# The product with the merged weights, as 36 matmuls a row tile or as seven products of quarter sums

## The chip, the cores and the metric

The kernel runs on one core of a Trainium2 chip. The metric is the device time of one execution in microseconds (us). The time before is 789.17 us, the median of three runs (788.98 to 789.34).

## The reference, cut to what matters

Three layers follow one another: an attention between 512 tokens and 32 state rows for each of 8 batches, a maximum of three products, and an exponential gate with a layer norm.

```python
scores = scale * np.matmul(x, state.transpose(0, 1, 3, 2))        # softmax(scores) @ state -> xread
...                                                               # the same the other way -> sread
x = np.ascontiguousarray(attn_out.transpose(0, 2, 1, 3)).reshape(B * S, H * D)
h = np.maximum(np.maximum(x @ w1, x @ w2), x @ w3)                # 512 -> 768
x = h @ w_out                                                     # 768 -> 512
h = x @ w_in                                                      # 512 -> 1024
e = np.exp(h - h_max)
sm = e / (np.sum(e, axis=-1, keepdims=True) + 1e-09)
solu = h * sm
ln = (solu - mu) / np.sqrt(var + 1e-06) * g_ln
return (ln @ w_out).astype(np.float32)                            # 1024 -> 512
```

Inputs and output are float32 (the weights come as float64 words and are cut down in the kernel). There are 4352 rows: 8 batches of 512 tokens, and 256 state rows.

## The kernel before, in words

Each float32 factor of a product is held as two float16 parts, a high part and the rest, and a product takes three matmuls (high-high, high-rest, rest-high: the pairs in `HL`). The two middle weights are merged first: W' = moe_w_out @ w_in, 768x1024, held in `Wp` as 6 slices `f` of 128 rows. So each row of h goes through one product with W' instead of two.

A batch goes through these steps. **Attention** (`x_*`, `sc_*`, `sn_*`): x is loaded into `xr` (one buffer), squared for its scale, split (`xh`), transposed by DMA (`xT`), multiplied with the state (`cP`, L288), and turned into attention weights `A` by a run of VectorE, ScalarE and GpSimd instructions (L298 to L375, the tiles `T`, `e2`, `A32`). **h**: for each of the 6 slices `f` the state times w1 to w3 is built (`uP`, L725, evacuated into `SW` at L731 and L734), and three matmul groups of six, one for each weight, give h (`hP`, L747). ScalarE scales the first (`hA`, L756), VectorE takes the maximum with the others (`hV`, `hW`, L762), ScalarE and GpSimd write the two float16 parts into `hT` (`hB`, L773, and `hG`, L777). **z**: for each of the 4 row tiles of 128 rows, `zP` (L805) runs 36 matmuls of 128x512 (6 slices, 3 pairs of parts, 2 column halves) into a double PSUM bank. Then come the row maximum on VectorE (`zM`, L814), the exponential on ScalarE (`zE`, L822), the product on VectorE (`zG`, L834), a square sum on ScalarE (`zQ`, L848), a small root on GpSimd (`zH`, L855 to L858), the high part on ScalarE (`zA`, L862), the normed value on VectorE (`zB`, L866), the rest on VectorE (`zC`, L871) and a DMA transposition (`zT`, L876). **Output**: `OP` (L886) runs 24 matmuls a tile, `OA` (L893) takes them out of PSUM and `OL` (L903) stores them. The 256 state rows go the same way as two tiles called `s`.

The order of all engines is written out by hand. `ORDER` is a string of words such as `zP:12` (step `zP`, batch 1, tile 2; in `hP:15` batch 1, slice 5), and every engine runs its instructions in the order in which the words stand:

```python
    with tc.manual_schedule():
        for word in ORDER.split():
            step(word)
```

Each engine waits in that order, so one waiting instruction holds all behind it. SP issues every load, store and transposition. PSUM has 8 banks: four single ones and two double ones (`bank`, `wide`). SBUF buffers that several steps share go by tag: `e` (6 buffers, for exponentials and weights in conversion), `hT`, `xr`, `hm`.

Of the kernel before, what the change touches and what calls it, by code (L numbers as in the profile page):

```python
# [981 lines left out]
```

## Time and profile before

| what | value |
|---|---|
| median of 3 runs | 789.17 us |
| the profiled execution | 788.87 us, its span 787.0 us |
| granted TensorE clock | 0.998 of full speed |
| TensorE busy | 761.6 us (97% of the span) |
| VectorE busy | 476.5 us (61%) |
| ScalarE busy | 383.3 us (49%) |
| GpSimd busy | 167.4 us (21%) |
| moved by DMA | 70.54 MB |

The profile of one execution gives a page (busy time of each engine, groups of instructions with their mean duration, DMA issues), and views of the trace: busy time in chosen windows, the chain of work that ended last, who waited for whom, and the instructions in order of time. The span is the time between the first and the last instruction of the core. The execution's own time is 1.9 us longer.

### The profile page before, as it was taken

To read this page: it belongs to the slowest core of one execution; us is meant where nothing else is said; L and a number is where in the kernel's file an instruction comes from. 1 tells how busy PE (TensorE), PEld (TensorE's weight loads), DVE (VectorE), ACT (ScalarE), POOL (GpSimd) and SP (SyncE) were. 2 spreads that over 40 slices of the span, in tenths; PEclk is the share of its full clock that TensorE was granted. 3 is DMA by queue.
4 is the path that set the end of the run, shared out by engine and by line. 5 is a ranking of instruction groups with operands and counts; after the bars stand their busy time and mean duration, and the time that the engine had idled before them with its cause. 6 is when DMAs were issued, how large, how long until landed. Compare 5 with 4: busy or idle time off the path is not lost.

```text
span 787.0 us, 12487 instructions
## 1 busy us (share of the span) xinstructions
PE 761.6 (97%) x5094; PEld 362.2 (46%) x5094; DVE 476.5 (61%) x840; ACT 383.3 (49%) x611; POOL 167.4 (21%) x222
## 2 busy tenths in 40 slices
PE   3898999999999999999999999999999999999998
PEld 1444444444444444444444444444444476444444
DVE  4689999986556546573755763647655534345261
ACT  5867768755345343644455444534543433153062
POOL 0012343133122220221211320223132112022020
PEclk9999999999999999999999999999999999999999
DMA  9997361430524131570451134610450401321144
GB/s 340 340 264 242 70 161 22 83 99 1 95 54 95 41 81 28 120 162 1 80 137 26 41 60 75 147 27 2 81 121 1 68 1 41 55 54 27 40 86 116
DMA packets 146729, 70.54 MB, mean 90 GB/s; under 512 B 127088, under 2 KB 135536, under 8 KB 146160
## 3 DMA queue, kind: packets, MB, share of 16 engines
q1 hardware_dynamic: 146672, 69.75, 37.3%
q8 instruction: 40, 0.66, 0.3%
q14 instruction: 17, 0.14, 0.1%
HBM read 29.89 MB, written 8.91 MB: 49 GB/s over the span
## 4 chain that ended last, share of the span: by engine, by line
PE 81%; DVE 8%; ACT 5%; DMA 3%; issue 1%; SPq 0%; POOL 0%; ACTq 0%; DVEq 0%; POOLq 0%
PE z L805 29%; PE o L886 21%; PE h L747 20%; PE hs L789 3%; PE sw L725 3%; PE zs L805 2%; DMA xr<-in_x_dram 2%; DVE cv L453 1%; PE os L886 1%; DMA raw<-in_moe_w_dram 1%; PE pr L388 1%; DVE Wt L649 1%; ACT cv L435 1%; ACT junk L462 1%; DVE SW L734 1%
## 5 line engine op out<-in xcount | busy, mean ns | idle before, releaser
L805 PE MATMUL z<-Wp,hT 128*128 128x512 f16 x1152 | 252.8, 379 | 0.0
L747 PE MATMUL h<-A,SW 128*128 128x512 f16 x864 | 192.6, 379 | 1.4 <-ACT SW L731 0.5
L805 PEld LDWEIGHTS <-hT 128*128 128x128 f16 x1152 | 111.9, 98 | 135.9 <-issue 2.5
L886 PE MATMUL o<-Wo,ln 128*128 128x512 f16 (+2 forms) x792 | 169.8, 373 | 0.4 <-DVE zsm L827 0.4
L747 PEld LDWEIGHTS <-SW 128*128 128x128 f16 x864 | 82.4, 98 | 103.8 <-issue 6.6
L886 PEld LDWEIGHTS <-ln 128*128 128x128 f16 x840 | 80.8, 98 | 95.5 <-issue 1.2
L777 POOL TENSOR_TENSOR hT<-hm,hT 128x512 f16<-128x512 f32 x48 | 59.5, 1248 | 190.7 <-ACT hT L773 173.7
L762 DVE SCALAR_TENSOR_TENSOR hm<-h,phi,hm 128x512 f32<-128x512 f32 x96 | 71.2, 747 | 38.5 <-ACT hm L756 35.6
L731 ACT ACTIVATE SW<-sw 128x384 f16<-128x384 f32 x96 | 44.4, 486 | 74.7 <-PE sw L725 56.9
L814 DVE TENSOR_REDUCE zmx<-z 128x1 f32<-128x1024 f32 x32 | 39.1, 1222 | 66.6 <-PE z L805 66.5
L734 DVE SCALAR_TENSOR_TENSOR SW<-sw,SW 128x384 f16<-128x384 f32 x96 | 51.8, 548 | 38.2 <-ACT SW L731 38.1
L822 ACT ACTIVATE e<-z,zmx,beta_x 128x1024 f32<-128x1024 f32 x32 | 38.5, 1202 | 70.0 <-DVE zmx L815 68.4
L893 ACT ACTIVATE ob<-o,gamma 128x512 f32<-128x512 f32 (+2 forms) x33 | 22.2, 672 | 102.5 <-PE o L886 90.1
L756 ACT ACTIVATE hm<-h,phi 128x512 f32<-128x512 f32 x48 | 32.8, 684 | 44.7 <-PE h L747 39.8
L855 POOL TENSOR_SCALAR rs<-rs 128x1 f32<-128x1 f32 x34 | 9.8, 289 | 208.5 <-ACT ln L848 208.5
L575 PE MATMUL wp<-Wo,Wp 128*128 128x512 f32 x96 | 46.5, 641 | 0.8 <-DVE Wo L453 0.8
L871 DVE TENSOR_TENSOR ln<-e,ln 128x1024 f16<-128x1024 f32 x34 | 44.3, 1306 | 0.3
L866 DVE TENSOR_SCALAR e<-e,mean,rs 128x1024 f32<-128x1024 f32 x34 | 30.5, 903 | 22.6 <-ACT ln L862 22.6
L862 ACT ACTIVATE ln<-e,nb,rs 128x1024 f16<-128x1024 f32 x34 | 41.9, 1235 | 3.4 <-POOL nb L858 3.4
L848 ACT ACTIVATE ln<-e,mean 128x1024 f16<-128x1024 f32 x34 | 38.8, 1143 | 9.6 <-DVE mean L837 6.0
L834 DVE SCALAR_TENSOR_TENSOR e<-z,zsm,e 128x1024 f32<-128x1024 f32 x32 | 40.9, 1279 | 0.6
L773 ACT CAST hT<-hm 128x512 f16<-128x512 f32 x48 | 29.1, 613 | 21.3 <-DVE hm L762 11.4
(151 smaller groups left out, 712.9 us busy)
## 6 DMA issues: line engine op xcount, KB each, us to landing
xr<-in_x_dram SPq DMA_DIRECT2D x8, 1024.0 KB, 6.4
out_dram<-ob SPq DMA_DIRECT2D x31, 256.0 KB, 3.2
raw<-in_moe_w_out_dram SPq DMA_DIRECT2D x5, 1024.0 KB, 6.0
raw<-in_moe_w_dram SPq DMA_DIRECT2D x4, 1024.0 KB, 12.2
Wt<-in_moe_w_dram SPq DMA_DIRECT2D x3, 1024.0 KB, 9.4
Wt<-in_moe_w_in_dram SPq DMA_DIRECT2D x2, 1024.0 KB, 7.1
raw<-in_moe_w_in_dram SPq DMA_DIRECT2D x2, 1024.0 KB, 10.1
raw_h<-in_moe_w_dram SPq DMA_DIRECT2D x2, 1024.0 KB, 10.0
```

The source lines that it names most:

```text
L575: nc.tensor.matmul(zs[f][:, c * HALF:(c + 1) * HALF], a1T[f][:, e], b1[:, e, c * HALF:(c + 1) * HALF], start=e == 0, stop=e == NE - 1)
L731: nc.scalar.activation(sw_t[b, f][:, 0, g], sw_t[b, f, g][:, :3 * P], AF.Copy, scale=2.0 ** -18)
L734: nc.vector.scalar_tensor_tensor(out=sw_t[b, f][:, 1, g], in0=sw_t.pop((b, f, g))[:, :3 * P], scalar=2.0 ** -18, in1=sw_t[b, f][:, 0, g], ...
L747: nc.tensor.matmul(parts[w], SW[:, u, g, w * P:(w + 1) * P], A[:, v, g, :], start=n == 0, stop=n == 3 * NG - 1)
L762: nc.vector.scalar_tensor_tensor(out=c, in0=h_t[b, f][i], scalar=phi[f // 2][:, i:i + 1], in1=c, op0=ALU.mult, op1=ALU.max)
L777: nc.gpsimd.tensor_tensor(out=h_t[b][:, 1, f, :n], in0=c_t.pop((b, f)), in1=h_t[b][:, 0, f, :n], op=ALU.subtract)
L805: nc.tensor.matmul(z[:, c * HALF:(c + 1) * HALF], h_t[b][:, u, f, t * P:(t + 1) * P], Wp[:, v, f, c * HALF:(c + 1) * HALF], start=n == 0, ...
L814: nc.vector.tensor_reduce(out=d["mx"], in_=d["z"], axis=AX.X, op=ALU.max)
L834: nc.vector.scalar_tensor_tensor(out=d["e"], in0=d["z"], scalar=d["sm"], in1=d["e"], op0=ALU.mult, op1=ALU.mult, accum_out=mu)
L862: nc.scalar.activation(d["ln"][:, 0, 0], d["e"], AF.Identity, bias=d["nb"], scale=d["rs"])
L871: nc.vector.tensor_tensor(out=d["ln"][:, 0, 1], in0=d["e"], in1=d["ln"][:, 0, 0], op=ALU.subtract)
L886: nc.tensor.matmul(d["po", c.start], lT[:, u, k, :], Wo[:, v, k, c], start=n == 0, stop=n == 3 * NK - 1)
```

## The change

For the batches 1 to 7 and for the state rows, z = h W' is no longer made tile by tile. h is taken as four quarters (even and odd slices `f`, first and second tile of a pair of row tiles `u`), W' as four quarters (even and odd slices, left and right 512 columns), and seven products of sums of quarters (`Y`, 9 matmuls of 128x512 each, into one bank) are added up to the four quarters of z. Batch 0 keeps the 36 matmuls a tile.

The words of the new steps: `j` sums of quarters of h on VectorE, `jA` and `jG` their two float16 parts on ScalarE and GpSimd; `t*` the sums of W', once, on GpSimd, ScalarE and VectorE, kept in `Ts` and in the upper right quarter of `Wp`; `Y:bui` product i of pair u of batch b; `K` the copy of product 1 into SBUF on ScalarE; `V` the additions on VectorE, the last one for each quarter with a row maximum; `wD` and `wR` write the converted w1 to w3 to DRAM and bring one third of them back for each batch, since `Ts` takes the room of one third.

Core of the diff (`ORDER` is written anew, with 1941 words for 1489; of it one line of each version stands here):

```diff
-zM:40 zE:40 eA:50 eA:51 zP:41 zR:40 uV:511 xP:6 zG:40 OL:31 n2:5 n3:5 eW:51 uA:500 uA:510 zM:41 n4:5
+uV:530 Y:406 hG:45 jG:400 jA:420 jG:420 uA:520 Y:403 Y:414 Y:405 K:40 Y:402 uV:520 zA:33 n3:5 zB:33
...
-    def bank(name):
-        return ps.tile([P, 512], F32, tag="bank", name=name, bufs=4)
-
-    def wide(name):
-        return ps.tile([P, 1024], F32, tag="wide", name=name, bufs=2)
+    free, held = list(range(8)), {}
+
+    def bank(name, uses=1):
+        k = free.pop(0)
+        t = ps.tile([P, 512], F32, tag=f"bank{k}", name=name)
...
+    def w_keep(q):
+        nc.sync.dma_start(out=W_mem[q], in_=Wq(0, q).rearrange("p v a i c -> p (v a i c)"))
+
+    def w_fetch(b):
+        q = order_q[b][2]
+        nc.sync.dma_start(out=Wq(b, q).rearrange("p v a i c -> p (v a i c)"), in_=W_mem[q])
...
-    NE4 = 6
+    NE4 = 5
...
+        half = NG * S
+        att_s[b] = {"xr": xr.rearrange("p (a j r d) -> p a j r d", a=NPR, j=2, d=D),
+                    "T": xr[:, :half].rearrange("p (g c n) -> p g c n", g=NG, n=N),
+                    "e2": xr[:, half:].rearrange("p (g s) -> p g s", g=NG), "A": xr[:, half:]}
...
+    def h_sum(b, q, i):
...
+        x, y, op = (lambda: (even(0), even(1), ALU.subtract), lambda: (even(1), odd(1), ALU.add),
+                    lambda: (t[:, 1], even(0), ALU.subtract), lambda: (odd(0), t[:, 2], ALU.subtract))[i]()
+        nc.vector.tensor_tensor(out=t[:, i], in0=x, in1=y, op=op)
...
+    TSUM = nc.gpsimd
...
+    def t_diff(q):
+
+        t = ts_t[q] = t_tile(q, "t32")
+        TSUM.tensor_tensor(out=t, in0=both(q, 1, 1), in1=both(q, 0, 1), op=ALU.subtract)
...
+    def y_mm(b, u, i):
+
+        y_t[b, u, i] = bank(f"y{b}_{u}_{i}", 2 if i == 5 else 1)
+        j, place = PRODUCTS[i]
+        n = 0
+        for q in range(NQ):
+            for v, w in HL:
+                nc.tensor.matmul(y_t[b, u, i], h_t[b][:, v, q, j, u * P:(u + 1) * P], place(w, q),
+                                 start=n == 0, stop=n == 3 * NQ - 1)
+                n += 1
...
+    SUMS = {6: (1, 0, 6, False), 2: (0, 0, 2, True), 7: (2, 1, 7, False), 8: (3, 2, 5, True),
+            5: (1, 1, 5, False), 3: (1, 1, 3, True), 4: (2, 2, 4, True)}
+
+    def y_add(b, u, i):
+
+        k, j, n, last = SUMS[i]
+        out_, x, y = z_half(b, u, k), z_half(b, u, j), y_t[b, u, n]
+        if last:
+            mh = z_t[b, 2 * u + k // 2]["mh"]
+            nc.vector.tensor_tensor_reduce(out=out_, in0=x, in1=y, scale=1.0, scalar=-3.0e38, op0=ALU.add,
+                                           op1=ALU.max, accum_out=mh[:, k % 2:k % 2 + 1])
+        else:
+            nc.vector.tensor_tensor(out=out_, in0=x, in1=y, op=ALU.add)
+        used(y)
...
     def z_norm(b, t):
         d = z_t[b, t]
-        nc.vector.tensor_scalar(out=d["e"], in0=d["e"], scalar1=d["mean"][:, 0:1], scalar2=d["rs"],
-                                op0=ALU.add, op1=ALU.mult)
+        nc.scalar.activation(d["e"], d["e"], AF.Identity, bias=d["nb"], scale=d["rs"])
```

Three places in the order show it. First VectorE in the middle of the run, at the gate of batch 3. `A32_4` belongs to the attention of batch 4, `z3_0` is the product of batch 3, tile 0; the last number of a name is its buffer. Before:

```order
L365 STREAM_TRANSPOSE A32_4_3642<-T4_3493 128x1024
L814 TENSOR_REDUCE zmx_3709<-z3_0_3604 128x1
L815 TENSOR_SCALAR zmx_3709<-zmx_3709,beta_x_93 128x1
L827 TENSOR_SCALAR zsm_3713<-zsm_3713,s_beta_x_950 128x1
L829 RECIPROCAL zsm_3713<-zsm_3713 128x1
L834 SCALAR_TENSOR_TENSOR e_3712,mu_3746<-z3_0_3604,zsm_3713,e_3712 128x1024
L837 TENSOR_SCALAR mean_3748<-mu_3746 128x1
L838 TENSOR_SCALAR mean_3748<-mu_3746 128x1
```

After, at the same place (`y3_0_6` is product 6 of pair 0 of batch 3, `zb` a row tile of z in SBUF):

```order
L1054 TENSOR_TENSOR zb_3876<-zb_3876,y3_0_6_3910 128x512
L1054 TENSOR_TENSOR zb_3945<-zb_3876,y3_0_7_3888 128x512
L1054 TENSOR_TENSOR zb_3876<-zb_3876,y3_0_5_3935 128x512
L831 SCALAR_TENSOR_TENSOR SW4_1_3696<-sw4_1_0_3697,SW4_1_3696 128x384
L831 SCALAR_TENSOR_TENSOR SW4_1_3696<-sw4_1_1_3698,SW4_1_3696 128x384
L1051 ISA zb_3945,zmh_3946<-zb_3945,y3_0_5_3935 128x512
L1051 ISA zmh_3946 128x1
L1051 ISA zb_3876,zmh_3877<-zb_3876,y3_0_3_3922 128x512
L1051 ISA zmh_3877 128x1
L1051 ISA zb_3945,zmh_3946<-zb_3945,y3_0_4_3964 128x512
L1051 ISA zmh_3946 128x1
L1137 TENSOR_TENSOR ln_3814<-e_3611,ln_3814 128x1024
```

The row maximum over 1024 columns (`L814`) is gone; the additions of the products stand in its place, and four of the seven carry a row maximum of 512 columns with them (`L1051`, and a row that reads it out).

Second GpSimd, in the stretch between batch 0's z and batch 1's. Before, it holds the softmax of batch 1 (`T`, `A`), the roots (`rs`, `nb`) and the rest parts of h (`hT`):

```order
L359 TENSOR_TENSOR T_1061<-T_1061,rn 128x1024
L708 TENSOR_SCALAR gamma<-p_o 128x1
L375 TENSOR_TENSOR A_1341<-A_1_1309,A_1341 128x1024
L262 TENSOR_SCALAR al_1380<-p_x_1375,p_s 128x1
L855 TENSOR_SCALAR rs<-rs 128x1
L856 TENSOR_TENSOR rs<-rs,mhalf 128x1
L858 TENSOR_TENSOR nb<-mean,rs 128x1
L777 TENSOR_TENSOR hT_1550<-hm,hT_1550 128x512 x2
```

After, the sums of W' (`t_`) stand there, between the same steps:

```order
L939 TENSOR_TENSOR t_1448<-Wp 128x1024
L943 TENSOR_TENSOR t_1420<-t_1420 128x512
L947 TENSOR_TENSOR t_1420<-t_1420,Wp 128x512
L334 TENSOR_SCALAR al_1519<-p_x_1514,p_s 128x1
L943 TENSOR_TENSOR t_1448<-t_1448 128x512
L947 TENSOR_TENSOR t_1448<-t_1448,Wp 128x512 x2
L947 TENSOR_TENSOR t_1420<-t_1420,Wp 128x512
L1122 TENSOR_SCALAR rs<-rs 128x1
L1123 TENSOR_TENSOR rs<-rs,mhalf 128x1
L1125 TENSOR_TENSOR nb<-mean,rs 128x1
L958 TENSOR_TENSOR t_1448<-Wp,t_1448 128x512 x2
L939 TENSOR_TENSOR t_1678<-Wp 128x1024
```

The GpSimd queue gains 24 such instructions up to the end of batch 1's products, and the rest parts of h stand behind some of them.

Third ScalarE at the end, in the last tiles of batch 7 (`z_3` is the last tile, `os` the output of the state rows). Before:

```order
L862 ACTIVATE ln<-e,nb,rs 128x1024
L848 ACTIVATE ln,rs<-e,mean 128x1024
L893 ACTIVATE ob<-os_7423,gamma 128x512
L862 ACTIVATE ln<-e,nb,rs 128x1024 x2
L822 ACTIVATE e,zsm<-z_3_7489,zmx,beta_x 128x1024
L893 ACTIVATE ob<-os_7547,gamma 128x512
L848 ACTIVATE ln,rs<-e,mean 128x1024
L862 ACTIVATE ln<-e,nb,rs 128x1024
```

After:

```order
L1074 ACTIVATE e,zsm<-zb,zmx,beta_x 128x1024
L1115 ACTIVATE ln,rs<-e,mean 128x1024
L1074 ACTIVATE e,zsm<-zb,zmx,beta_x 128x1024
L1129 ACTIVATE ln<-e,nb,rs 128x1024
L1133 ACTIVATE e<-e,nb,rs 128x1024
L1115 ACTIVATE ln,rs<-e,mean 128x1024 x2
L1129 ACTIVATE ln<-e,nb,rs 128x1024
L1133 ACTIVATE e<-e,nb,rs 128x1024
L1074 ACTIVATE e,zsm<-zb,zmx,beta_x 128x1024
L1159 ACTIVATE ob<-os_7945,gamma 128x512
```

ScalarE now also writes the normed value (`L1133`), once a tile, and three tiles of batch 7 go through it together, ahead of the state rows' output.

## Rows read from the trace of the kernel before

**Rows 1.** The page, part 1: engine, busy us, share of the span, instructions.

```profile
PE 761.6 (97%) x5094; PEld 362.2 (46%) x5094; DVE 476.5 (61%) x840; ACT 383.3 (49%) x611; POOL 167.4 (21%) x222
```

**Rows 2.** Windows of 20 us: length, busy us of each engine; sum of 300 to 460.

```profile
60.00:80.00 20.00, 16.22 (x117) 8.19 (x116) 19.76 (x28) 13.48 (x17) 4.96 (x2) 0.91 0.72 247
...
120.00:140.00 20.00, 20.00 (x128) 9.37 (x127) 18.61 (x42) 17.96 (x31) 5.45 (x7) 1.00 0.14 27
140.00:160.00 20.00, 19.92 (x171) 9.27 (x168) 18.94 (x31) 14.01 (x25) 2.84 (x6) 1.00 0.51 103
...
sum 160.00, PE 159.48 PEld 72.78 DVE 97.35 ACT 75.03 POOL 35.41; mean PE 19.93 PEld 9.10 DVE 12.17 ACT 9.38 POOL 4.43
```

**Rows 3.** TensorE's waits, the longest: us in total, times, longest.

```profile
PE at L564 <- DVE cv L453: 11.9, 2, 6.8
```

**Rows 4.** The chain that ended last, in order of time: start, us, what.

```profile
293.07 1.40 PE pr L388 x48
...
341.39 0.77 PE sc L288 x24
...
342.84 7.88 PE h L747 x36
350.72 15.54 PE z L805 x72
366.26 1.10 PE sw L725 x48
...
744.84 5.18 PE os L886 x24
```

**Rows 5.** Groups by line and shape: busy us, mean ns, idle before.

```profile
L762 DVE SCALAR_TENSOR_TENSOR hm<-h,phi,hm 128x512 f32<-128x512 f32 x96 | 71.2, 747 | 38.5 <-ACT hm L756 35.6
L777 POOL TENSOR_TENSOR hT<-hm,hT 128x512 f16<-128x512 f32 x48 | 59.5, 1248 | 190.7 <-ACT hT L773 173.7 <-PE h L747 16.9
L871 DVE TENSOR_TENSOR ln<-e,ln 128x1024 f16<-128x1024 f32 x34 | 44.3, 1306 | 0.3
L862 ACT ACTIVATE ln<-e,nb,rs 128x1024 f16<-128x1024 f32 x34 | 41.9, 1235 | 3.4 <-POOL nb L858 3.4
L814 DVE TENSOR_REDUCE zmx<-z 128x1 f32<-128x1024 f32 x32 | 39.1, 1222 | 66.6 <-PE z L805 66.5
L866 DVE TENSOR_SCALAR e<-e,mean,rs 128x1024 f32<-128x1024 f32 x34 | 30.5, 903 | 22.6 <-ACT ln L862 22.6
L773 ACT CAST hT<-hm 128x512 f16<-128x512 f32 x48 | 29.1, 613 | 21.3 <-DVE hm L762 11.4 <-PE zs L805 6.5 <-PE z L805 3.3
L893 ACT ACTIVATE ob<-o,gamma 128x512 f32<-128x512 f32 x31 | 21.2, 685 | 98.5 <-PE o L886 86.1 <-DMA out_dram<-ob 7.1 <-issue 5.0
L343 POOL TENSOR_TENSOR T<-T,mxn 128x1024 f32<-128x1024 f32 x8 | 17.1, 2138 | 34.4 <-DVE mxn L339 34.4
L762 DVE SCALAR_TENSOR_TENSOR hm<-hs,phi,hm 128x256 f32<-128x256 f32 x12 | 5.7, 480 | 17.5 <-ACT hm L756 16.6 <-PE hs L789 0.8
```

**Rows 6.** Single lines: duration in ns min/median/max, first and last start.

```profile
L834 DVE SCALAR_TENSOR_TENSOR e<-z,zsm,e x32: 1243/1283/1285, 122.6 to 763.4; 128x1024 f32<-128x1024 f32 x32
L834 DVE DVE_READ_ACCUMULATOR e<-z,zsm,e x32: 77/83/85, 123.8 to 764.6; 128x1 f32 x32
...
L871 DVE TENSOR_TENSOR ln<-e,ln x34: 1203/1218/2827, 152.8 to 769.5; 128x1024 f16<-128x1024 f32 x34
...
L777 POOL TENSOR_TENSOR hT<-hm,hT x48: 1150/1157/2160, 93.4 to 718.2; 128x512 f16<-128x512 f32 x48
```

**Rows 7.** DMA issues: size in KB, median us from issue to landing.

```profile
xr<-in_x_dram SPq DMA_DIRECT2D x8, 1024.0 KB, 6.4
...
ln<-ln SPq DMA_TRANSPOSE x34, 4.4
```

**Rows 8.** In order of time: batch 2's load issued, its attention weights finished.

```profile
107.82 0.48 SPq L238 DMA_DIRECT2D xr<-in_x_dram  x1
...
188.81 2.12 POOL L375 TENSOR_TENSOR A<-A,A 128x1024 f16<-128x1024 f32 x1 [4.55 <-ACT A L370]
```

More of the change, by code (lines that the diff above doesn't have):

```diff
@@ L257, in x_scale @@
         m = tiny.tile([P, 1], F32, name="xm2")
[L258 removed]
+        pt = t.pop("row")
+        nc.vector.tensor_reduce(out=m, in_=pt[:, :P], axis=AX.X, op=ALU.max)
+        used(pt)
         p = xs_p[b] = root(m, f"x{b}")
@@ L566, in turned @@
     def turned(f):
-        nc.scalar.copy(a1T[f], at.pop(f).rearrange("p (e c) -> p e c", c=P))
+        nc.scalar.copy(a1T[f], at[f].rearrange("p (e c) -> p e c", c=P))
+        used(at.pop(f))
     def prod(f, *es):
         if f not in zs:
-            zs[f] = wide(f"wp{f}")
+            zs[f] = [bank(f"wp{f}_{c}", 2) for c in range(2)]
         for e in es:
             for c in range(2):
-                nc.tensor.matmul(zs[f][:, c * HALF:(c + 1) * HALF], a1T[f][:, e],
+                nc.tensor.matmul(zs[f][c], a1T[f][:, e],
                                  b1[:, e, c * HALF:(c + 1) * HALF], start=e == 0, stop=e == NE - 1)
@@ L623, in st_scale @@
         m = tiny.tile([P, 1], F32, name="stm2")
-        nc.vector.tensor_reduce(out=m, in_=row.pop("st"), axis=AX.X, op=ALU.max)
+        pt = row.pop("st")
+        nc.vector.tensor_reduce(out=m, in_=pt[:, :P], axis=AX.X, op=ALU.max)
+        used(pt)
         root(m, "st", p_s)
@@ new lines, in t_four, with t_four2, t_four_hi, t_four_lo @@
+    def t_four(q):
+        t = ts_t[q, 4] = t_tile(q, "t4")
+        TSUM.tensor_tensor(out=t, in0=both(q, 1, 0), in1=Ts[:, :, q, 1], op=ALU.subtract)
+    def t_four2(q):
+        t = ts_t[q, 4]
+        TSUM.tensor_tensor(out=t[:, 0], in0=t[:, 0], in1=t[:, 1], op=ALU.add)
+    def t_four_hi(q):
+        nc.scalar.copy(W4(0, q, 0, 1), ts_t[q, 4][:, 0])
+    def t_four_lo(q):
+        nc.vector.tensor_tensor(out=W4(1, q, 0, 1), in0=ts_t[q, 4][:, 0], in1=W4(0, q, 0, 1),
+                                op=ALU.subtract)
@@ L780, in hs_mm @@
+    ts_t, hs_t = {}, {}
     def hs_mm(f):
-        z = wide(f"hs{f}")
-        y = bank(f"hs2_{f}")
         n = B * N
-        parts = [z[:, :n], z[:, 512:512 + n], y[:, :n]]
+        parts = [bank(f"hs{f}_{w}") for w in range(3)]
         for w in range(3):
@@ L799, in z_mm @@
         d = z_t[b, t] = {}
-        z = d["z"] = wide(f"z{b}_{t}")
+        z = d["z"] = [bank(f"z{b}_{t}_{c}", 3) for c in range(2)]
         n = 0
@@ new lines, in z_half, with y_out @@
+    def z_half(b, u, i):
+        d = z_t.setdefault((b, 2 * u + i // 2), {})
+        if "z" not in d:
+            d["z"] = mm.tile([P, F2], F32, tag="e", name="zb", bufs=NE4)
+            d["mh"] = tiny.tile([P, 2], F32, name="zmh")
+        return d["z"][:, i % 2 * HALF:(i % 2 + 1) * HALF]
+    def y_out(b, u):
+        nc.scalar.copy(z_half(b, u, 0), y_t[b, u, 1])
+        used(y_t[b, u, 1])
+    SUMS = {6: (1, 0, 6, False), 2: (0, 0, 2, True), 7: (2, 1, 7, False), 8: (3, 2, 5, True),
+            5: (1, 1, 5, False), 3: (1, 1, 3, True), 4: (2, 2, 4, True)}
@@ L881, in o_mm @@
         lT = d["ln"][:, 1].rearrange("p e (k c) -> p e k c", c=P)
-        d["po", c.start] = bank(f"o{b}_{t}")[:, c]
+        d["po", c.start] = bank(f"o{b}_{t}")
         n = 0
```

467 lines of the change are left out of this document (309 added, 158 removed).

## The prediction

> **What bounds the kernel now.** I read the page's part 1 first: TensorE is busy for 761.6 of 787.0 us, VectorE for 476.5, ScalarE for 383.3, GpSimd for 167.4 [rows 1]. Then the windows of 20 us, since an average over stages can mislead. The loss of TensorE sits at the start: it waits 11.9 us for its first converted weights [rows 3], and in 60 to 80 us it is busy for 16.22 of 20 while VectorE is at 19.76, so there the weight conversion sets the pace [rows 2]. From then on TensorE is full. The reader should look at 120 to 160 us: VectorE is at 18.61 and 18.94 of 20, and TensorE still at 20.00 and 19.92 [rows 2]. So a VectorE that is 94% busy can keep TensorE fed in this order. In the steady part (300 to 460 us) VectorE needs 97.35 of 160 us, 61%, and TensorE has 159.48 [rows 2]. Last the chain in order of time: from the middle on it is a row of matmul groups without gaps [rows 4]. What counts is therefore how much matmul time goes, and whether the other engines keep up.
>
> **Matmuls removed.** Before, a pair of row tiles took 2 x 36 matmuls for z; after, 7 x 9 = 63. There are 14 pairs in batches 1 to 7 and one of state rows: 1080 matmuls become 945. In the chain 72 of z took 15.54 us, 0.2158 each; 36 of h, which change the bank after every six, took 7.88, 0.2189 each [rows 4]. The seven products change the bank after nine. Between these two rows, a change costs 6 x 0.0031 = 0.019 us, so one of nine costs 0.2158 + 0.0021 = 0.2179. Then 1080 x 0.2158 = 233.1 becomes 945 x 0.2179 = 205.9: **-27.2 us** (ends -29.1 and -26.2 at the two rows' prices).
>
> **VectorE.** The maximum over a tile goes for 30 tiles (30 x 1.222 = 36.7 us) and the normed value for 34 (30.5 us) [rows 5]. Added are 105 additions, each with one input in PSUM and one in SBUF as in the maximum of h, 0.747 [rows 5]: 78.4. Sixty carry a maximum and a read-out of 0.083 [rows 6]: 5.0. Then 96 sums of h of 256 columns at 0.48 at most [rows 5]: 46; and 8 for the rests of the sums of W'. Sum 476.5 - 67.2 + 137 = 547 of some 766 us, 71%. In one batch it is +8.5 us (10.5 + 0.7 + 5.8 - 8.5) on 61% of the batch. A batch of TensorE is 4 z tiles (31.1), 4 output tiles (20.7), 6 slices of h (23.6), their state products (3.3) and 2.2 for attention, 80.9 us [rows 4], and becomes 77.3: so 49.2 + 8.5 = 58 of 77.3, 75%. That is under the 94% at which TensorE was still fed, so it costs **0**. The addition with a maximum is a form that the trace doesn't show: from 0.65 (half of a 1024-column two-input row, 1.306) to 1.5, twice the row of h's maximum. I take 0.747, nearest in inputs and width. At 1.5 it is 45 us more, 77%, still covered.
>
> **ScalarE and GpSimd.** ScalarE gains the normed value (34 x 1.235 = 42), the copy of product 1 (15 x 0.685) and the high parts of the sums of h (48, mostly 0.613) [rows 5], less half of 24 casts: some 82 us, 466 of 766, 61%. GpSimd gains 48 rest parts at up to 1.248, 24 sums of W' (six of 1024 columns at 2.138, eighteen of 512 at 1.248: 35 us) and loses half of 24: 248 of 766, 32% [rows 1, 5]. Averages cost **0**; two stretches do not follow the average.
>
> **The sums of W'.** They stand on GpSimd between batch 0's last z tile and batch 1's last products, and the products with summed weights wait for them. From the first sum to the last, the queue holds 27 instructions of 512 columns (18 sums, 9 rest parts of h), seven of 1024, three of 256 (0.7) and three roots (1.1): 33.7 + 15.0 + 2.1 + 3.3 = 54 us [rows 5]. TensorE has in that stretch one z tile (7.8), six slices of h (23.6) with state products and scores (4.1), two output tiles (10.4) and twelve of the fourteen products (23.5): 70 us [rows 4]. So 16 us are spare. But rows 6 show a collision: the product line, which reads z from PSUM, takes 1283 ns at the median and 1285 at most; the rest line L871, with both inputs in SBUF, 1218 at the median and 2827 at most; GpSimd's rest of h 1157 and 2160. VectorE has about 20 us of instructions with two SBUF inputs in this stretch (12 sums of h, the sums' rests, the splits). If none of them overlaps GpSimd, 54 + 20 = 74, 4 us more than TensorE has, and the last sum still passes ScalarE and VectorE (2 us): +6. If they overlap as mostly before: 0. I take the middle, **+3**, since most of these lines run at their median. [...]
>
> **The end.** Four tiles of batch 7 finish almost together, under two state output tiles (2 x 5.18) and their own. Let 0 be the end of the last product. The second pair's product 3 ends at -1.9; VectorE is then in the product line of another tile (1.3) and has the maximum ready at 2.2. The exponential of that tile stands ahead of tile 0's high part on ScalarE, so tile 0 goes: exponential to 3.6, high part to 4.8, normed value to 6.0, the rest on VectorE (1.3, behind an addition) to 7.8, transposition 4.4 [rows 7] to 12.2. The state output tiles end at 10.4: **+1.8**. The next three tiles come at about 16.8, 22.1 and 27.0, for slots at 17.4, 22.6 and 27.8. Ends: 0, and +5 if each of ten ScalarE rows starts late by half of its length.
>
> **Moved or at nothing.** The writes and fetches of w1 to w3 (11 of 1.5 MB) stand on SP between transpositions; a load of 1 MB lands in 6.4 us [rows 7], and between the last use of a third and its next lie over 30 us of matmuls. At the start VectorE gets twelve half conversions of W' for six whole ones, +1 us, and the loads stand in another order; the 3.8 us that TensorE loses in 60 to 80 us may vanish or double: 0, ends -3.8 and +3.8. A wait is added: `T`, `e2` and `A` now lie in `xr`, so the load of the next x waits for the end of this batch's attention; behind it on SP stand transpositions of z. That is the second rival.
>
> **Sum.** 788.9 (the profiled execution; the median of the runs is 0.3 higher, which I leave in the range) - 27.2 + 3 + 1.8 + 0 = **766.5 us**. With all ends: 788.9 - 29.1 - 3.8 = 756 to 788.9 - 26.2 + 6 + 5 + 3.8 = 777.5; its own range, not all ends at once, is 757 to 774.
>
> **Rival 1: GpSimd sets the pace of batch 1's products.** The mechanism is the collision above, in full, and GpSimd also waits for ScalarE as it does now, 190.7 us before 48 rest parts, 4.0 each [rows 5]. With three such waits 54 + 20 + 12 + 2 = 88 us stand against 70: 18 late, 788.9 - 27.2 + 18 + 1.8 = **781.5**. Against it: much of that waiting is only for lack of work. [...] Chance 0.14, for 774 to 787.
>
> **Rival 2: the attention loop becomes the bound; slower.** Load of x, square, split, transposition, scores, softmax, `A`, next load is now a closed ring, once a batch. Bare it is 6.4 + 4.4 us [rows 7] and some 16 instructions of 1.2 to 2.1, about 35 us of 77.3. But its instructions stand in full queues: before, batch 2 took from its load at 107.82 to the end of `A` at 190.93, 83.1 us [rows 8], without harm because loads ran ahead. If the ring takes 83.1, six rings cost 6 x 5.8 = 35: 788.9 - 27.2 + 35 = **797**. From 77.3 a ring it costs time, from 77.3 + 27.2 / 6 = 81.8 the kernel is slower than before. Against it: the order is new, and the load stands right behind the attention's end. Chance 0.11.
>
> **Rival 3: better than the sum.** Every cover holds and the start loses its 3.8 us: **756** or less. Chance 0.09.
>
> **How the numbers follow.** Forecast 0.62, rivals 0.14, 0.11 and 0.09; 0.04 for a mixture that ends within 0.2% of the time before, about what a measurement can tell from no change. Faster 0.62 + 0.14 + 0.09 = 0.85, same 0.04, slower 0.11. The range of 755 to 784 holds the forecast, most of rival 1 and half of rival 3, some 0.8.
>
> **What would show it.** Right: 135 matmuls fewer, a TensorE busy time of 733 to 736 us, nearly no idle time from 120 us to the last 30 us, VectorE near 545, ScalarE near 465, GpSimd near 250. The sums of W': TensorE's wait at the first products with `Ts` is under 6 us. The end: a wait of some 2 us ahead of batch 7's first output tile. Wrong: gaps in every batch ahead of h (rival 2), a gap of over 10 us in batch 1's products (rival 1), a product above 0.219 us a matmul, or additions with a maximum far above 0.75 us.

## The result, and the profile after

The changed kernel took **763.1 us** (median of 4 runs, 762.6 to 765.0) beside 789.2 us of the kernel before: a ratio of 0.967, with an interval of 0.9657 to 0.9691. The profiled execution shown here took 762.59 us. The prediction was 766.5 us with a range of 755 to 784. Of the 26.3 us between the two profiled executions, 30.4 come from TensorE's busy time (761.6 to 731.2 us) and 4.1 are lost again to its idle time (25.4 to 29.5 us, span less busy).

The page, part 1, of the kernel after, as in [rows 1]: engine, busy us, share of the span, instructions.

```profile
PE 731.2 (96%) x4959; PEld 350.8 (46%) x4959; DVE 541.6 (71%) x1072; ACT 458.0 (60%) x731; POOL 253.4 (33%) x297
```

5094 - 4959 = 135 matmuls are gone, and the other engines' totals stand within 8 us of what was foreseen (547, 466 and 248 us).

Windows of 20 us of the kernel after, as in [rows 2]: length, busy us of PE, PEld, DVE, ACT, POOL, then the granted clock as a share of full, the DMA share and GB/s.

```profile
60.00:80.00 20.00, 12.13 (x152) 7.47 (x151) 19.07 (x32) 14.22 (x17) 1.52 (x4) 0.90 0.51 146
80.00:100.00 20.00, 18.94 (x169) 8.80 (x169) 17.88 (x37) 14.24 (x22) 6.65 (x14) 0.84 0.56 207
...
140.00:160.00 20.00, 18.94 (x147) 7.73 (x146) 18.74 (x43) 16.16 (x26) 15.32 (x17) 1.00 0.28 108
160.00:180.00 20.00, 19.68 (x176) 8.78 (x175) 19.14 (x37) 11.53 (x24) 14.55 (x12) 1.00 0.95 200
...
240.00:260.00 20.00, 17.20 (x143) 7.65 (x142) 17.01 (x31) 12.04 (x22) 5.97 (x8) 1.00 0.38 78
...
320.00:340.00 20.00, 20.00 (x137) 9.06 (x136) 17.04 (x37) 13.46 (x25) 10.81 (x10) 1.00 0.18 41
```

Read the third number of each line, TensorE's: 20.00 in every window from 260 to 740 us (the last line stands for them), though VectorE now does 17 of 20 there. What is lost lies in three places: the start (60 to 100 us, where the granted clock is low too), the sums of W' (140 to 180 us, 1.4 us of idle time) and one gap at 240 to 260 us.

The chain that ended last, in order of time, as in [rows 4]: start, us, engine and group.

```profile
242.21 5.93 DMA ln<-ln
248.19 5.35 PE o L1152 x24
253.54 7.77 PE h L843 x36
...
271.58 15.54 PE y L1026 x72
...
345.41 17.59 PE y L1026 x81
...
699.33 27.20 PE y L1026 x126
726.52 10.36 PE os L1152 x48
736.88 20.80 PE o L1152 x120
```

72 matmuls of the products take 15.54 us as 72 of z did; 126 take 27.20, which is 0.2159 each. (The 81 at 345.41 take 0.11 us more than 81 x 0.2158 = 17.48: they stand right behind a row of state products, and the part on the prediction comes back to that.) At 248.19 an output tile starts only when its transposition has landed. At the end nothing stands between the state output tiles and the last five groups.

Single lines of the kernel after, as in [rows 6]: duration in ns as min/median/max, first and last start.

```profile
L1051 DVE CUSTOM_DVE_ANT_0 zb<-zb,y x56: 646/680/689, 206.6 to 730.3; 128x512 f32<-128x512 f32 x56
L1054 DVE TENSOR_TENSOR zb<-zb,y x42: 628/683/689, 201.1 to 722.8; 128x512 f32<-128x512 f32 x42
L1097 DVE SCALAR_TENSOR_TENSOR e<-zb,zsm,e x30: 1273/1284/2252, 226.9 to 737.4; 128x1024 f32<-128x1024 f32 x30
L1097 DVE SCALAR_TENSOR_TENSOR e<-z,zsm,e x8: 734/745/749, 129.7 to 172.8; 128x512 f32<-128x512 f32 x8
```

An addition costs 0.68 us with or without the maximum. The product line is the same instruction in both its rows: where its z still lies in PSUM (batch 0) no execution is longer than 749 ns; where the products put z into SBUF, one takes up to 2252 ns. That is new: before, with z in PSUM, the longest took 1285 [rows 6]. The one of 2252 starts at 695.95 us, within 0.02 us of a GpSimd row of 1.15 us.

### The profile page after: what moved, and what is told of

Read it like the earlier page. It is cut to its first block, busy times and chain, and to the rows that moved or that the text cites. A ratio compares the mean times of both kernels' runs of the same rounds, so it can differ in the third digit from the quotient of the medians.

```text
span 760.7 us, 12727 instructions
## 1 busy us (share of the span) xinstructions
PE 731.2 (96%) x4959; PEld 350.8 (46%) x4959; DVE 541.6 (71%) x1072; ACT 458.0 (60%) x731; POOL 253.4 (33%) x297
## 4 chain that ended last, share of the span: by engine, by line
PE 73%; DVE 13%; DMA 5%; ACT 2%; POOL 2%; issue 2%; SPq 1%; DVEq 0%; ACTq 0%
PE y L1026 22%; PE o L1152 21%; PE h L843 20%; PE hs L991 3%; PE sw L821 3%; PE ys L1026 2%; DMA raw_h<-in_moe_w_out_dram 2%; DVE hm L859 2%; PE os L1152 1%; DVE cv L535 1%; DMA raw_h<-in_moe_w_dram 1%; PE pr L459 1%; DVE cv L525 1%; DMA xr<-in_x_dram 1%; DVE xh L351 1%
## 5 line engine op out<-in xcount | busy, mean ns | idle before, releaser
L1026 PEld LDWEIGHTS <-hT 128*128 128x128 f16 x882 | 85.8, 98 | 103.7 <-issue 1.3
L1026 PE MATMUL y<-Wp,hT 128*128 128x512 f16 x504 | 114.5, 379 | 0.0
L897 POOL TENSOR_TENSOR hT<-hm,hT 128x512 f16<-128x512 f32 (+1 forms) x48 | 52.6, 1106 | 109.3 <-ACT hT L893 93.7
L1026 PE MATMUL y<-Ts,hT 128*128 128x512 f16 x378 | 85.8, 379 | 0.0
L921 POOL TENSOR_TENSOR hT<-hs,hT 128x512 f16<-128x512 f32 x42 | 53.9, 1298 | 26.0 <-ACT hT L918 26.0
L1054 DVE TENSOR_TENSOR zb<-zb,y 128x512 f32<-128x512 f32 x42 | 28.3, 679 | 41.2 <-PE y L1026 37.1
L1122 POOL TENSOR_SCALAR rs<-rs 128x1 f32<-128x1 f32 x34 | 12.4, 366 | 129.1 <-ACT ln L1115 129.1
L1074 ACT ACTIVATE e<-zb,zmx,beta_x 128x1024 f32<-128x1024 f32 x28 | 34.6, 1236 | 33.4 <-DVE zmx L1065 28.5
L1051 DVE CUSTOM_DVE_ANT_0 zb<-zb,y 128x512 f32<-128x512 f32 x56 | 37.4, 680 | 12.5 <-PE y L1026 12.1
L1133 ACT ACTIVATE e<-e,nb,rs 128x1024 f32<-128x1024 f32 x34 | 42.0, 1238 | 0.4
```

The lines of the kernel that those rows point to most:

```text
L897: nc.gpsimd.tensor_tensor(out=h_part(b, f, 1)[1], in0=src, in1=hi, op=ALU.subtract)
L921: nc.gpsimd.tensor_tensor(out=h_sum_at(b, q, 1, i), in0=hs_t[b, q][:, 2 * i:2 * i + 2], in1=h_sum_at(b, q, 0, i), op=ALU.subtract)
L1026: nc.tensor.matmul(y_t[b, u, i], h_t[b][:, v, q, j, u * P:(u + 1) * P], place(w, q), start=n == 0, stop=n == 3 * NQ - 1)
L1133: nc.scalar.activation(d["e"], d["e"], AF.Identity, bias=d["nb"], scale=d["rs"])
```

## Experiments

Twelve kernels ran. Each was timed against the kernel before; the kernel after has 0.967 on that scale. TensorE's waits stand in the rows in brackets: us, and what ended the wait.

### The matmuls alone, and everything else alone

The first leaves 135 matmuls out of the kernel before; the second puts 135 back into the kernel after.

```diff
 # before, z_mm
+    full = 3 * NF if b == 0 else 3 * NF - 2 - (t % 2 and c)
+    if n >= full:
+        continue
 # after, y_mm
+    for again in range(2 if i == 1 else 1):
         n = 0
         for q in range(NQ):
```

> The kernel before, with 9 of the 72 matmuls of each pair of z tiles left out (the last ones of w', two or three of 36 in each half; 15 pairs, 135 matmuls); nothing else is touched. It measures the matmuls alone. Theory, TensorE's time is the kernel's time: 135 x 0.2158 = 29.1 us less, 760.0, and TensorE's idle time stays near the 25 us of before. Rival, VectorE, which is 94% busy from 120 to 160 us, can't follow a faster TensorE: part of the gain comes back as idle time there, 763 to 768. The term of 27.2 us in the prediction would be too small by 1.9 in either case if the products of nine cost no more than 0.2158 each.

> The kernel after, with product 1 of each pair run twice into its bank (9 matmuls more for each of 15 pairs, so 72 as before; the result is the same). It measures everything in the change but the matmuls. Theory, the additions, sums and moves are hidden but for the start: 763.1 + 29.1 = 792.2, that is 3 us over the kernel before. Rival, the other engines pace some stretch of the kernel after, and longer matmul work hides that: 787 to 789, no slower than before. If the added work had cost nothing at all, it would be 789.2.

**Measured:** 764.0 us (ratio 0.9681, 0.9667 to 0.9695), so 24.7 us less than the kernel before, which took 788.7 beside it; and 790.8 us (ratio 1.0022, 1.0012 to 1.0032), so 27.7 us more than the kernel after. The page, part 1, of the first and then of the second:

```profile
PE 733.6 (96%) x4959; PEld 348.7 (46%) x4959; DVE 475.4 (62%) x840; ACT 383.5 (50%) x611; POOL 169.7 (22%) x222
```

```profile
PE 760.7 (97%) x5094; PEld 364.7 (46%) x5094; DVE 540.1 (69%) x1072; ACT 458.2 (58%) x731; POOL 252.9 (32%) x297
```

135 matmuls are worth 28.0 and 29.5 us of busy time, as 135 x 0.2158 = 29.1 says, but 24.7 and 27.7 us of the kernel's time. In the first case the order is the one made for longer products, and waits come up that were not there: idle time goes from 25.4 to 28.5 us, 2.2 of it in the timeline row below. So taking matmuls out of an order that was fitted to them gives back some of the gain. How much of the kernel after's time is owed to its new order no run shows: its own idle time is 29.5 us. The second figure says that all the work that the change adds costs 1.7 us of 789 (0.22%) when the matmuls stay. Between theory (792) and rival (787 to 789) it lies nearer to the theory.

TensorE's timeline in the kernel before with 63 matmuls a pair: start, us, group, and in brackets the wait ahead of it.

```profile
316.89 5.35 PE L889 MATMUL o<-Wo,ln 128*128 128x512 f16 x24 [2.21 <-DMA ln<-ln]
```

### The ring of attention

```diff
-        nc.sync.dma_start(out=xr..., in_=x[b]...)
+        for again in range(2 if b > 1 else 1):
+            nc.sync.dma_start(out=xr..., in_=x[b]...)
```

> The kernel after, with the load of x issued twice into its place for batches 2 to 7, so that the closed ring of attention (load, square, split, scores, softmax, A, next load) becomes longer by one transfer of 1 MB, some 6.4 us by the rows of before. Theory, the ring has slack in every batch, since TensorE has no idle time from 260 to 740 us: 763 to 765. Rival, each load starts at the very end of the attention before it, so the ring has no slack and is only just not the bound: six rings x 6.4 = 38 us more, 801.

**Measured:** 773.3 us (ratio 0.9802, 0.9784 to 0.9821), 10.2 us more. Neither theory nor rival. First the kernel after, where the ring can be read: GpSimd ends `A` (L446), SP issues the next load (L303).

```profile
129.79 2.14 POOL L446 TENSOR_TENSOR A<-xr,A 128x1024 f16<-128x1024 f32 x1
131.95 0.37 SPq L303 DMA_DIRECT2D xr<-in_x_dram  x1
...
212.45 2.13 POOL L446 TENSOR_TENSOR A<-xr,A 128x1024 f16<-128x1024 f32 x1 [2.46 <-ACT A L441]
217.41 0.57 SPq L303 DMA_DIRECT2D xr<-in_x_dram  x1
```

Batch 2's load is issued at 131.95, 0.02 us after the end of batch 1's `A`; its own `A` ends at 214.58, 82.6 us later, more than the 81.8 from which the prediction let the kernel become slower. (Batch 3's load follows 2.8 us after that end; a transposition stands before it on SP.) Then the doubled load, timeline of ScalarE and TensorE:

```profile
144.43 1.91 ACT L320 ACTIVATE xh<-xr 128x2048 bf16<-128x2048 f32 x1 [6.00 <-DMA xr<-in_x_dram]
...
147.06 0.80 PE L249 MATMUL pb_x<-ident,xm 128*128 128x128 f32 x2 [5.10 <-ACT hm L853]
...
237.40 0.49 PE L249 MATMUL pb_x<-ident,xm 128*128 128x128 f32 x2 [2.50 <-ACT xh L320]
```

Two of six rings have less than one load of slack: batch 2's (TensorE waits 5.1 us) and batch 3's (2.5 us). From batch 4 on the second load of each ring, 5.7 us from issue to landing, costs TensorE nothing. The waits are 7.6 us; the rest is matmuls at a low clock behind them (busy time 734.8 for 731.2 us; granted clock 0.94 from 120 to 180 us and 0.93 from 240 to 260, where the kernel after has 1.00).

### The normed value back on VectorE: in all tiles, then in the middle only

```diff
-        nc.scalar.activation(d["e"], d["e"], AF.Identity, bias=d["nb"], scale=d["rs"])
+        nc.vector.tensor_scalar(out=d["e"], in0=d["e"], scalar1=d["mean"][:, 0:1], scalar2=d["rs"],
+                                op0=ALU.add, op1=ALU.mult)      # second kernel: if b in (2, 3, 4, 5, 6)
```

> The kernel after, with the normed value back on VectorE, as a subtraction of the mean and a multiplication (34 x 0.90 = 30.5 us by the rows of before), off ScalarE (34 x 1.24 = 42 us). VectorE goes from 541.6 to 572 us, 75% of the run. Theory of the prediction, an engine below 94% in a stretch costs nothing: 763 to 764, and the wait of 2.6 us ahead of an output tile at 248 us, which follows a late normed value on ScalarE, goes or moves. Rival, VectorE is full from 100 to 180 us (18.7 to 19.9 of 20 in each window) and the four tiles of batch 0 there add 3.6 us to what TensorE waits for: 766 to 768.

> The kernel after, with the normed value on VectorE in batches 2 to 6 only (20 of 34 tiles, 18 us more for VectorE); batches 0, 1, 7 and the state rows keep it on ScalarE. In the run with all 34 on VectorE the long waits stood at 159, 252 and 750 to 758 us, those of 262 to 740 us came to 1.4 us. Theory, the loss lies in the stretches where VectorE is full (100 to 180 us) or where a single tile's steps follow one another without other work (the end), and not in the mean: 763 to 766. Rival, any step that goes from ScalarE to VectorE lengthens each tile's way and costs in proportion, 20/34 of the 17.5 us: 773.

**Measured:** 780.6 us (ratio 0.9885, 0.9853 to 0.9916) for all 34 tiles, 17.5 us more than the kernel after; 766.9 us (ratio 0.9727, 0.9712 to 0.9742) for the 20 tiles of batches 2 to 6, 3.8 us more. Page, part 1, and TensorE's timeline with all tiles on VectorE:

```profile
PE 742.0 (95%) x4959; PEld 353.4 (45%) x4959; DVE 569.7 (73%) x1106; ACT 420.1 (54%) x697; POOL 257.2 (33%) x297
```

```profile
158.97 0.68 PE L821 MATMUL sw<-Wa,sT 64*32 64x384 f16 x23 [2.44 <-ACT hm L852]
...
254.90 7.04 PE L1153 MATMUL o<-Wo,ln 128*128 128x512 f16 x24 [2.04 <-DMA ln<-ln]
...
749.77 5.35 PE L1153 MATMUL o<-Wo,ln 128*128 128x512 f16 x24 [1.38 <-DMA ln<-ln]
758.66 18.48 PE L1153 MATMUL o<-Wo,ln 128*128 128x512 f16 x96 [3.54 <-DMA ln<-ln]
```

VectorE at 73% of the span costs 17.5 us by the medians. The execution shown took 782.1 us, 19.5 more than that of the kernel after: 8.7 us more idle time of TensorE and 10.8 us more busy time for the same 4959 matmuls, at a granted clock that is down to 0.66 from 160 to 170 us and 0.79 from 760 to 770. Past the start, the waits of over 1 us stand near 160 us, where VectorE is busy for 18.4 and 18.1 of 20 us (140 to 180), near 250 us, where the kernel after waits too, and at the end, where VectorE is busy for 6.2 of 15 us (745 to 760) and a tile's steps follow one another. In the middle only three waits, of 0.5, 0.9 and 0.2 us, are left, which the second kernel has too. The second kernel's 3.8 us are below a proportional share (20/34 x 17.5 = 10.3) and outside the theory's 763 to 766 by 0.9. In its execution shown (769.2 us) TensorE's idle time is that of the kernel after (29.6 us for 29.5), so the 20 rows added no wait in all; the 6.6 us that it took longer are busy time, 2.9 of them one output tile at a low clock, which the last section shows. Some 0.6 us are lost ahead of all rows that were moved, since batch 0's z starts at 112.78 us for 112.19.

### The sums of W'

The first puts the 24 sums on VectorE, the second leaves all but 8 columns of 512 of them out (and fills a part of their room once, on GpSimd, with a constant).

```diff
-    TSUM = nc.gpsimd
+    TSUM = nc.vector
 # the other kernel
-        t = ts_t[q] = t_tile(q, "t32")
+        t = ts_t[q] = t_tile(q, "t32")[:, :, :FEW]      # FEW = 8, and so in all sums, casts and rests
```

> The kernel after, with the 24 sums of W' on VectorE, not on GpSimd: 6 of 1024 columns and 18 of 512, some 6 x 1.2 + 18 x 0.68 = 19.5 us more for VectorE between 135 and 205 us, where it is 17 of 20 us busy, and 33 us less for GpSimd. Theory, as with the normed value: VectorE's queue there is on the path, TensorE waits and its clock falls behind the wait, 8 to 20 us more, 771 to 783. Rival, GpSimd's 15 to 17.6 us of 20 there and its collisions with VectorE are the bound, and VectorE does the sums faster: 761 to 764.

> The kernel after, with the sums of W', their high parts and rests over 8 columns of 512 only (the rest of their places holds what was there, so the products with summed weights are other numbers). It is the price of the sums. Theory, they are hidden: TensorE waits 1.4 us in all from 140 to 180 us, so 761.5 to 763.5. Rival, the prediction's +3 us, spread over waits too short to see: 760.

**Measured:** 769.9 us (ratio 0.9767, 0.9746 to 0.9789), 6.8 us more; and 761.5 us (ratio 0.9652, 0.9638 to 0.9667), 1.6 us less than the kernel after. One window of 80 us, 130 to 210, of the sums on VectorE and then of the kernel after:

```profile
130.00:210.00 80.00, 74.09 (x511) 32.48 (x510) 76.86 (x145) 52.24 (x89) 23.25 (x25) 0.96 0.45 130
```

```profile
130.00:210.00 80.00, 78.63 (x547) 35.35 (x545) 70.16 (x130) 52.87 (x90) 60.66 (x52) 1.00 0.46 129
```

In the kernel after GpSimd has 60.7 of 80 us there and TensorE hardly waits; with the sums on VectorE, VectorE is at 96%, and TensorE loses 4.5 us more and has a granted clock of 0.96 for 1.00. The direction was the theory's, its size (8 to 20) too large. The kernel without sums shows their price: 1.6 us by the medians, though the two intervals overlap, and at the edge between its theory and its rival. Its trace shows more where the sums stand. It starts batch 0's z 0.45 us ahead of the kernel after (111.74 for 112.19), the first product 2.6 us ahead (184.42 for 187.01) and the output tile of 248.19 2.8 us ahead, at 245.42, so the sums cost 2.3 us on the way; 1.7 go back, since that tile then runs at a low clock (7.04 for 5.35 us):

```profile
245.42 7.04 PE L1154 MATMUL o<-Wo,ln 128*128 128x512 f16 x24 [2.59 <-DMA ln<-ln]
```

### The gap at 248 us

The first moves one word; the second moves a dozen words between 228 and 254 us.

```diff
 # e6
-zT:12 OP:12 uA:210 jA:210 hP:25
+zT:12 uA:210 jA:210 hP:25 OP:12
 # e11
-OP:01 xV:3 zA:12 zB:12 zC:12 hP:20 j:212 zE:13 zR:13 hG:22 uP:25 hA:20 zB:11 hV:20 zG:13 OA:01 uA:250 ...
+hP:20 xV:3 zA:12 zB:12 zC:12 uP:25 j:212 hA:20 uA:250 hV:20 zE:13 uA:251 zR:13 hG:22 uV:251 hW:20 OP:01 uV:250 zB:11 zG:13 OA:01 ...
-OP:12 uA:210 jA:210 hP:25
+uA:210 jA:210 hP:25 OP:12
```

> The kernel after, with one word moved: the output tile that waits 2.6 us for its transposition at 248 us now stands behind the next h group (4.0 us). Theory, the wait is a mere place in the order: 2.5 us less, 760.6. Rival, the h group waits there for its state product's rest on VectorE or the bank of the waiting output tile holds something else up: no difference, 763.

> The kernel after, with the stretch from 228 to 254 us in another order: slice 0 of h stands between the two output tiles there, its state products' weights and VectorE's rests for the next slice stand ahead of a normed value and a product line, and the output tile that waited 2.6 us stands behind the next h group. Theory, TensorE's wait there goes: 760.5. Rival, as with the output tile alone moved, VectorE and ScalarE are late with the h group instead: 763 to 767.

**Measured:** 767.4 us (ratio 0.9727, 0.9710 to 0.9743), 4.3 us worse, and 761.6 us (ratio 0.9654, 0.9639 to 0.9668). TensorE's timeline with the one word moved, then with the stretch in another order:

```profile
250.84 6.31 PE L838 MATMUL h<-A,SW 128*128 128x512 f16 x16 [4.23 <-DVE SW L826]
```

```profile
246.13 0.59 PE L838 MATMUL h<-A,SW 128*128 128x512 f16 x2 [0.65 <-DVE SW L826]
247.26 3.63 PE L838 MATMUL h<-A,SW 128*128 128x512 f16 x16 [0.53 <-DVE SW L826]
250.72 5.34 PE L1147 MATMUL o<-Wo,ln 128*128 128x512 f16 x24
```

The tile that waited 2.6 us was cover for an h group that is not ready before 250.8 us: its state products' rest stands late in VectorE's queue. Moved alone, the tile uncovers a wait of 4.2 us, and the 16 matmuls behind it take 6.31 us where they take 3.63 otherwise (granted clock 0.68 from 250 to 260 us). With the two engines' rows for that h group moved ahead as well, 0.65 + 0.53 us are left. That is the best of the kernels here that do all the work, 1.6 us under the kernel after by the medians, though the two intervals still overlap.

### The start

All three kernels give `A` of batch 0 a place in `Wo` and put the first h slices ahead of the last weight conversions; they differ in what stands behind. The third also has the order of e11.

```diff
-            t["A"] = mm.tile([P, NG * S], F32, tag="e", name="A32", bufs=NE4)
+            t["A"] = b1[:, 0]
 # words: A's transposition n5:0, n6:0, n7:0 and hP:01 move ahead of B:w21 .. B:w22, wG:2, wP:2
 # e10 also: wG:1 wP:1 wS:1 ahead of hP:01, xL:1 ahead of L:w22
 # e12 also: xQ:1 ahead of uP:03, xP:1 behind hP:02, hP:03 ahead of wP:2
```

> The kernel after, with the words from 55 to 100 us in another order: A of batch 0 gets a place of its own in Wo (free once the last product of w_in has run) in place of a buffer of the conversions, its transposition stands right behind the state products' weights of slices 0 and 1, and the first h slices stand ahead of the last weight conversions. The first h group can then start at 71 to 73 us, not at 82.4, and fill the 9 us that TensorE waits between 65 and 82 us. Theory, the start of the kernel after loses what it loses because TensorE waits there and is granted 0.84 to 0.90 of its clock afterwards: 756 to 760. Rival, VectorE (17.9 to 19.9 of 20 us busy in each window from 60 to 180 us) sets the pace of that whole stretch: what TensorE saves before 82 us it waits for before 180 us, 762 to 764.

> The kernel after, with A of batch 0 in Wo and the first h slices ahead of the last weight conversions, as in the run on the start before, but with the scales of the second third of w1 to w3 fetched ahead of the first h group (they stood behind it, and ScalarE was idle for 7.2 us, VectorE for 2.5 us) and with the load of the second x ahead of the last load of weights (TensorE waited 3.0 us for its square). Theory, the start can be shortened by what TensorE waits there: 757 to 761. Rival, VectorE, full from 60 to 180 us, gives none of it away: 763 to 766.

> The kernel after with both stretches in another order: the one from 228 to 254 us as in the run with slice 0 of h ahead, which took 761.6, and the start once more with A of batch 0 in Wo. In the last run on the start the first h groups ran from 76 us on, 6 us earlier than in the kernel after, but TensorE then waited 3.7 us for the square of the second x and 2.5 us for the last weights and their scales, and z started 3.8 us later than in the kernel after. Here the square stands in a gap of ScalarE and its sum behind two h groups, and slices 2 and 3 stand ahead of the last scales. Theory, the first 110 us lose by waits in the order: 756 to 760. Rival, VectorE sets their pace whatever the order: 761 to 763.

**Measured:** 766.1 us (ratio 0.9712, 0.9694 to 0.9731), 766.3 us (0.9712, 0.9695 to 0.9728) and 771.9 us (0.9778, 0.9764 to 0.9791): all slower than the kernel after. TensorE's timeline of the first, of the second, and of the third with the ScalarE row that explains it:

```profile
72.52 6.94 PE L838 MATMUL h<-A,SW 128*128 128x512 f16 x18 [1.92 <-DVE SW L826]
...
96.27 0.79 PE L244 MATMUL pb_x<-ident,xm 128*128 128x128 f32 x2 [3.00 <-ACT xh L314]
```

```profile
76.16 9.28 PE L838 MATMUL h<-A,SW 128*128 128x512 f16 x36
...
94.81 0.80 PE L244 MATMUL pb_x<-ident,xm 128*128 128x128 f32 x2 [3.68 <-ACT xh L314]
```

```profile
110.29 1.12 ACT L512 ACTIVATE cv<-raw 128x1024 f32<-128x1024 f32 x1 [8.58 <-DMA raw<-in_moe_w_out_dram]
...
111.84 10.48 PE L838 MATMUL h<-A,SW 128*128 128x512 f16 x36 [8.55 <-ACT SW L822]
```

The first h group does start 6 to 10 us earlier, as each theory said, but another wait comes up behind it each time: the square of the second x, and in the third kernel a conversion that stands ahead of state products on ScalarE while its load has not landed. Not all of the loss is waiting. In the first, TensorE's idle time is 31.5 us for 29.5, but its busy time 735.0 for 731.2, at a granted clock of 0.83 from 60 to 120 us for 0.91. These are faults of the orders that were tried, not a proof that VectorE sets the pace: the third has VectorE at 12.9 of 20 us from 100 to 120 us. Whether the start can be shortened stays open.

## Why the prediction was right, step by step

**What bounds it.** TensorE. After, it has 20.00 of 20 us in each window from 260 to 740 us; before, at least 19.56. Right.

**Matmuls, -27.2.** The count was right, the price was not. The step that failed is the cost of a bank change, 0.019 us, taken from the difference of the h and z rows [rows 4]. The products change the bank after nine matmuls and cost 0.2159 each, the price of z; h itself shows 7.77 us for 36 in the chain of after, also 0.2158. So the 0.0031 of h in [rows 4] was not a bank change. The chain of the kernel before shows both prices for z too, 7.88 right behind state products (`sw`) and 7.77 behind h:

```profile
273.74 1.10 PE sw L725 x48
274.84 7.88 PE z L805 x36
...
302.96 7.77 PE z L805 x36
```

The h row of [rows 4] also stands right behind state products, so its 0.11 us belong to its place, once a group, and not to its banks. The term is -29.1, 1.9 us more than predicted, and TensorE's busy time of 731.2 us lies below the 733 to 736 that were named as a sign of being right.

**VectorE and ScalarE, 0.** Right for this order, by luck in part, since the reason doesn't carry. The addition with a maximum costs 0.680, below the 0.747 chosen, and the total of 541.6 us is 5 less than worked out. But that 75% "is under the 94% at which TensorE was still fed, so it costs 0" is refuted by the kernel with 569.7 us on VectorE, 73% of its span, which lost 17.5 us, part of it by waits at the end, where VectorE is busy for 6.2 of 15 us. What counts is where the added rows stand: the kernel that moved only the 20 tiles in the middle lost 3.8 us, and in its trace no idle time was added.

**The sums of W', +3.** They cost 2.3 us in the trace of the kernel without them, 1.6 by the medians, so the size was near. The way was another. The prediction let products with summed weights wait for the last sum on GpSimd; none of them waits. TensorE's 1.4 us of idle time in 140 to 180 us stand ahead of z, h and its state products, on rows of ScalarE and VectorE:

```profile
155.84 0.68 PE L821 MATMUL sw<-Wa,sT 64*32 64x384 f16 x23 [0.38 <-ACT hm L852]
...
171.84 4.04 PE L843 MATMUL h<-A,SW 128*128 128x512 f16 x18 [0.32 <-DVE hm L859]
```

The collision of VectorE with GpSimd was read rightly for rows with two SBUF inputs. The Trainium skill, SBUF — State Buffer, "Who interferes with whom", has such a VectorE row contend with a GpSimd row that reads SBUF, and one with at most one SBUF input not, if it runs outside VectorE's 2-port modes. The trace agrees where the change made such a row out of another: the product line went from at most 1285 ns to at most 2252, while its eight executions on PSUM, each beside a GpSimd row, stayed at 749 at most (half the width) and the additions, with one input in PSUM, at 689. But rows with two SBUF inputs were not the only ones that were held up. The normed value of the kernel before, with one tile of SBUF as its input, took 2692 ns for a median of 806 when it started at 188.80 us, together with a GpSimd row; whether it ran in a 2-port mode no run shows. The single line as in [rows 6], then GpSimd's timeline:

```profile
L866 DVE TENSOR_SCALAR e<-e,mean,rs x34: 801/806/2692, 151.2 to 768.7; 128x1024 f32<-128x1024 f32 x34
```

```profile
188.81 2.12 POOL L375 TENSOR_TENSOR A<-A,A 128x1024 f16<-128x1024 f32 x1 [4.55 <-ACT A L370]
```

**The end, +1.8.** It cost nothing: the output tiles follow one another without a wait at 736.88. The step that failed is the wait for the maximum: tile 0's high part stands on ScalarE behind another tile's exponential, and that one waits for its maximum. The prediction put the addition of product 3 behind a product line on VectorE, with the maximum ready 2.2 us after the last product, which ends at 726.53. The addition ran ahead of that line (at 724.62 and 725.23 us), and the maximum was ready at 0.4. VectorE's timeline, then ScalarE's:

```profile
726.68 0.27 DVE L1065 TENSOR_SCALAR zmx<-zmh,minus_x 128x1 f32<-128x1 f32 x1
...
728.28 1.23 ACT L1129 ACTIVATE ln<-e,nb,rs 128x1024 f16<-128x1024 f32 x1
```

So the high part of the first tile, at 728.28, ended 3.0 us after the last product (the prediction had 4.8), and its rest on VectorE at 5.6 (7.8). With 4.4 us for the transposition [rows 7] the tile was there at about 10.0, just ahead of the slot at 10.4.

**The start, 0 (-3.8 to 3.8).** In total right, but by luck: the way wasn't foreseen. Batch 0's z starts at 112.19 us, at 110.07 before, with two groups of state products (0.68 and 0.67 us) ahead of it that came later before: 0.8 us late. On the way TensorE waits 7.9 us for converted weights (their sums of squares, `gr`), a time that before held a product of w_in, which now runs earlier; its first h group starts at 82.43 instead of 79.28 us and takes 5.94 instead of 4.04 us (granted clock 0.84 from 80 to 100 us, 1.00 before).

**Missed.** The gap of 2.6 us at 248 us stands in no term and no rival.

The terms as measured, -29.1 + 2.3 + 0 + 0.8 + 2.6 = -23.4, leave 2.9 of the 26.3 us between the two executions shown unassigned. Some 1.4 of that is TensorE's busy time behind the start of z (672.9 us before, 641.1 after): it fell by 31.8 us, of which the matmuls account for 29.1 and the two groups of state products for 1.35. Which rows gave the rest no run here shows. That the sum came within 3.4 us of the median is in part luck: the matmuls, the sums and the end came out 1.9, 0.7 and 1.8 us better than they were priced, and the gap at 248 us and the start, 2.6 and 0.8 us, were not priced.

**Rival 1** didn't come: GpSimd was at 15.3, 14.6 and 17.6 of 20 us from 140 to 200 us and no product waited for it. **Rival 2** was nearer than its chance of 0.11 sounds. The ring is closed: five of the six loads go out within 0.03 us of the end of `A`. From load to the end of `A` the rings took 82.6, 62.7, 74.4, 88.3, 79.7 and 88.0 us, so three of them are above the 81.8 that was named as the point at which the kernel becomes slower, and their mean, 79.3, is above the 77.3 from which a ring was to cost time. Yet TensorE has no idle time from 260 to 740 us. The rival failed because it charged each ring's excess over the mean batch to the kernel, while what TensorE needs from the ring was still early enough; only the rings of batches 2 and 3 had less slack than the 5.7 us of one more load. **Rival 3** didn't come: the start lost 0.8 us more and not 3.8 less.

## What to carry to other kernels

Price removed matmuls by the row of the same shape in the steady part, and expect a little less of it where the order was fitted to the old lengths. The share of busy time of a second engine tells neither safety nor cost: look for the stretches where it is full and for the places where one tile's steps run alone, and try the load there. A wait in a fixed order may be the cover of a later one, so move what the next group waits for together with it, on every queue.
